# A linear-attention and MLP kernel on one core: five early loads of weights wait for the second one ahead of them, and scaled k gets two lasting buffers

## The chip, the cores and the metric

The kernel runs on one core of one Trainium2 chip. The metric is device time in microseconds, from runs of the whole kernel. Five engines work side by side, each through its own instructions in order: TensorE (PE in the rows, with its weight loads as PEld), VectorE (DVE), ScalarE (ACT), GpSimd (POOL) and SyncE (SP), which issues nearly all DMA transfers here.

## The reference

Per batch (4) and head (8), with a state of 48 x 48 and 768 steps:

```python
for t in range(S):
    cur = np.einsum('bhd,bhe->bhde', u[None] * kt, vt)
    y[:, :, t] = np.einsum('bhd,bhde->bhe', rt, state + cur)
    state = w[None, :, :, None] * state + np.einsum('bhd,bhe->bhde', kt, vt)
...
xt = x.transpose(0, 2, 1)          # x: y with the heads side by side, [4, 768, 384]
h = xt @ U @ V                     # U [768, 32], V [32, 768]: mixes the tokens
u = x + h.transpose(0, 2, 1)
ch = np.maximum(u @ w_ch1, 0.0) @ w_ch2   # 384 -> 1536 -> 384
return (u + ch).astype(np.float32)
```

## The kernel before

**Attention in chunks.** The 768 steps of a batch are cut into 6 chunks of 128, 24 in all. For a chunk, k is scaled by powers of the decay (`ks`, L657 to L663, 8 heads padded from 48 to 64 columns), r and `ks` are turned by TensorE (`ptr`, `ptk`, L712) and scaled on the way out of PSUM (`rT` on VectorE L721, `kT` on ScalarE L727 or VectorE L733). Products of them (`pab`, L751), masked (`am`, L885), multiply v (`pav`, L787 and L793); the state `S` goes from half chunk to half chunk (`S` L913, decayed `SW` L922). The second half of a chunk waits for a one-element copy `seen` (L866) of the first. The step's own term is `dv`: r times k times u (POOL L669 and L671 in the first batch), summed per head (`dg`, VectorE L677) and multiplied by v (ScalarE L681, eight pieces a chunk). `x` (L892) is their sum. The chunks of the first batch come first and have nothing to stand beside.

**The seam.** Each finished chunk of the first batch is multiplied by U into a bank called `wake` (`wake<-x,Uf`, L344), and turned into `pu` (`pu<-ident,x`). When all six are there, the bank is cast to `Gs` (ScalarE L947, VectorE L948), `pu` gets the product of V and `Gs` (`pu<-V,Gs`), and `uTh` and `uTl` (ScalarE L1012, VectorE L1013) are the high and low parts of u for the MLP. Then come the MLP's matmuls (`p<-uTh,w1s` and so on), a group of 384 tokens at a time, with `hh` (ScalarE L1080) and `hl` (VectorE L1081), and the attention of later chunks between them. `wake<-ident` and `wake2<-ident` are fillers, matmuls whose result is not used; the planner puts them where it reckons TensorE would wait. An fp32 matmul stands as two rows (x2) in the trace.

**The weights.** U (1 load unit), V (2), w1 (12 blocks of 128 x 384) and w2 (12) come as 64-bit words; `unit` (L487) makes a load of 384 KB for such a block (`raw_...`, L502) and a conversion to fp32 on ScalarE (L522, L534) and VectorE (L525, L528), after which a cast (ScalarE L548) and a subtraction (VectorE or POOL L549) give high and low parts `w1s`, `w2s`. The load units come in the order u, v_0, v_1, w1_0_0, w1_1_0, w1_2_0, w2_0, w2_1, w2_2, w1_0_1, w1_1_1, w1_2_1, w2_3 and so on. r, k and v of a chunk come as loads of 192 KB (`ldr`, `ldk`, `ldv`, L618) and swapped halves of v (`vsw`, L630).

**What sets the order.** `Plan` (L47 to L273) records all operations with their reads and writes, and a list scheduler orders them on each engine by written-in costs: durations, when a DMA is reckoned to land (`LATE` = 2500 ns more for a load of weights), and how many rows are in flight. Engines then run in that order, waiting only for what they read or write. So a changed cost moves instructions on all engines. `ks` comes from a ring of two buffers (NK = 2), each with a memset of its padding on POOL:

```python
ks = kss[n] = wbuf([128, H, HP], F32, "ks", NK, f"ks_{n}")
op("POOL", 250, lambda: nc.gpsimd.memset(ks.t[:, :, D:], 0.0), [(ks, "pad")], [])
on_either(384, lambda e: e.tensor_mul(ks.t[:, :, :D], kt()[:, :, :D], by_head(tab.t)), [(ks, "d")], kb + [tab],
          only="DVE" if front(n) else None)
```

## Time and profile before

| | |
|---|---|
| Runs | 436.54, 437.32, 436.99 us; median 436.99 |
| Profiled execution, its own time | 439.95 us |
| Its span, first to last instruction | 437.9 us (2.05 us lie around it) |
| Mean granted TensorE clock | 0.984 of full |
| TensorE busy | 419.4 us, 96% of the span |
| VectorE busy | 267.8 us, 61% |
| ScalarE busy | 142.9 us, 33% |
| POOL busy | 55.6 us, 13% |

Busy shares are averages over stages with different limits, so what a change is worth is read from the chain of waits and from windows of the stage that it touches. The granted clock is given as a share of 2.4 GHz; its lower level, 1.2 GHz, is 0.50.

### The profile page before, as it was taken

How to read it: one execution, taken by the hardware profiler on the slowest of the kernel's cores; microseconds unless marked ns; L12 is line 12 of the kernel's file. 1: busy time of each engine (PE TensorE's matmuls, PEld its weight loads, DVE VectorE, ACT ScalarE, POOL GpSimd, SP SyncE). 2: the span in 40 equal slices, each digit the busy share in tenths (PEclk: the TensorE clock that was granted, in tenths of full speed). 3: DMA queues.
4: the chain of work that ended last, by engine and by line, in shares of the span. 5: the costliest groups of instructions: out<-in, count | busy, mean ns of one | idle time of the engine just before them, and what ended most of it. 6: DMA issues, size and time to landing. Idle time of an engine off the chain costs nothing.

```text
span 437.9 us, 12193 instructions
## 1 busy us (share of the span) xinstructions
PE 419.4 (96%) x5125; PEld 399.8 (91%) x5125; DVE 267.8 (61%) x602; ACT 142.9 (33%) x399; POOL 55.6 (13%) x92
## 2 busy tenths in 40 slices
PE   8889999999999999999999999999999999999991
PEld 8678899889999999999999999999999999999991
DVE  6979699999887757767775456567522351122121
ACT  1679679934421213121112221222112131111110
POOL 2651151223110002011100001101100000000000
PEclk9989699999999999999999999999999999999998
DMA  9979999654466876744586653231100510001001
...
DMA packets 178975, 43.93 MB, mean 100 GB/s; under 512 B 168993, under 2 KB 175650, under 8 KB 178914
## 3 DMA queue, kind: packets, MB, share of 16 engines
...
q10 hardware_dynamic: 4752, 0.89, 1.5%
q8 instruction: 42, 0.69, 0.7%
...
## 4 chain that ended last, share of the span: by engine, by line
PE 81%; DVE 8%; ACT 3%; DMA 3%; POOL 1%; issue 1%; SPq 0%; ACTq 0%; DVEq 0%; POOLq 0%
PE p L344 64%; PE pav L787 5%; PE pav L793 4%; PE pu L344 3%; DVE raw_w L528 2%; DVE raw_w L525 2%; PE pab L751 2%; DMA ld<-in_r_dram 1%; DMA ld<-in_v_dram 1%; PE pab L766 1%; PE wake L344 1%; DVE hl L1081 1%; PE pG L958 1%; ACT dv L681 1%; POOL dv L671 1%
## 5 line engine op out<-in xcount | busy, mean ns | idle before, releaser
L344 PE MATMUL p<-uTh,w1s 128*128 128x384 f32 x576 | 148.2, 338 | 0.0
L1081 DVE SCALAR_TENSOR_TENSOR hl<-p,hh 128x384 fp32r<-128x384 f32 x96 | 53.2, 554 | 119.3 <-ACT hh L1080 119.0
L344 PE MATMUL p<-w2s,hh 128*128 128x384 f32 x576 | 120.3, 340 | 0.6 <-ACT hh L1080 0.6
L1080 ACT ACTIVATE hh<-p 128x384 fp32r<-128x384 f32 x96 | 47.2, 491 | 210.3 <-PE p L344 208.7
L344 PEld LDWEIGHTS p<-uTh,w1s 128*128 128x128 f32 x576 | 102.9, 188 | 0.8
L344 PEld LDWEIGHTS p<-w2s,hh 128*128 128x128 f32 x576 | 99.8, 188 | 2.8 <-ACT hh L1080 0.9
L344 PE MATMUL p<-uTl,w1s 128*128 128x384 f32 x288 | 96.4, 335 | 0.0
L344 PE MATMUL p<-w2s,hl 128*128 128x384 f32 x288 | 65.8, 335 | 0.0
L344 PEld LDWEIGHTS p<-uTl,w1s 128*128 128x128 f32 x288 | 54.0, 188 | 0.0
L344 PEld LDWEIGHTS p<-w2s,hl 128*128 128x128 f32 x288 | 51.4, 188 | 0.0
L787 PE MATMUL pav<-vsw,am 64*64 64x48 f32 x384 | 33.0, 226 | 0.6 <-DVE am L885 0.5
L793 PE MATMUL pav<-S,rT 48*64 48x48 f32 x704 | 32.0, 222 | 0.9 <-issue 0.9
L787 PEld LDWEIGHTS pav<-vsw,am 64*64 64x64 f32 x384 | 26.7, 137 | 6.1 <-issue 4.1
L751 PE MATMUL pab<-rT,kT 48*64 48x64 f32 x768 | 31.2, 228 | 0.3 <-DVE rT L721 0.2
L793 PEld LDWEIGHTS pav<-S,rT 48*64 48x64 f32 x704 | 27.9, 139 | 1.0 <-issue 1.0
L751 PEld LDWEIGHTS pab<-rT,kT 48*64 48x64 f32 x768 | 25.1, 137 | 1.5 <-DVE rT L721 0.5
L787 PE MATMUL pav<-ldv,am 64*64 64x48 f32 x320 | 26.5, 222 | 0.0
L787 PEld LDWEIGHTS pav<-ldv,am 64*64 64x64 f32 x320 | 21.5, 134 | 4.7 <-issue 3.9
L885 DVE TENSOR_TENSOR am<-pab,mask 128x256 f32<-128x256 f32 x48 | 19.7, 417 | 6.8 <-PE pav L793 6.2
L661 POOL MEMSET ks<- 128x128 f32 x24 | 4.9, 205 | 133.2 <-PE pab L766 66.8
L766 PE MATMUL pab<-ldv,ks 64*48 64x48 f32 (+1 forms) x576 | 21.0, 212 | 0.0
L926 ACT ACTIVATE SW<-S,wm 112x48 f32<-112x48 f32 x48 | 12.2, 324 | 21.3 <-DVE S L913 20.0
...
## 6 DMA issues: line engine op xcount, KB each, us to landing
raw_w<-in_moe_w_ch_dram SPq DMA_DIRECT2D x24, 384.0 KB, 7.4
out_dram<-x SPq DMA_DIRECT2D x24, 192.0 KB, 2.0
ldr<-in_r_dram SPq DMA_DIRECT2D x20, 192.0 KB, 3.3
ldk<-in_k_dram SPq DMA_DIRECT2D x20, 192.0 KB, 3.6
ldv<-in_v_dram SPq DMA_DIRECT2D x20, 192.0 KB, 3.6
...
```

Of the source, the lines that this page charges most:

```text
L344: return nc.tensor.matmul(*args, **kw)
L525: nc.vector.scalar_tensor_tensor(word(0), word(1), -2 ** 31, word(0), ALU.bitwise_and, ALU.bitwise_or)
L528: nc.vector.scalar_tensor_tensor(word(0), word(1), 3, word(0), ALU.logical_shift_left, ALU.bitwise_or)
L661: op("POOL", 250, lambda: nc.gpsimd.memset(ks.t[:, :, D:], 0.0), [(ks, "pad")], [])
L751: return [lambda q=q, i=i: nc.tensor.matmul(pt.t[(i ^ j) * C2:(i ^ j) * C2 + C2, q * C2:(q + 1) * C2], lhsT=kT.t[rows, q, i * C2:(i + 1) * ...
L766: return nc.tensor.matmul(pt.t[j * HP:j * HP + m, SU + q * D:SU + (q + 1) * D], lhsT=ks.t[half, 2 * q + j, :m], rhs=vt()[half, 2 * q + j, ...
L787: return nc.tensor.matmul(to(q, j, i), lhsT=am[j].t[half, q, :], rhs=vsw[n].t[half, q, :] if j else vt()[half, 2 * q, :], start=(row == RO ...
L793: return nc.tensor.matmul(to(q, row, i), lhsT=rT.t[rows, q, i * C2:(i + 1) * C2], rhs=St[n, i].t[rows, q, :], start=False, stop=(row == RO ...
L885: on_dve(256, lambda e: e.tensor_tensor(am.t, abs_[n][j].t[:, :SU].rearrange("p (h t) -> p h t", h=NP), mask_.unsqueeze(1).broadcast_to([1 ...
L926: nc.scalar.activation(dec.t[:, q], new.t[:, q], AF.Copy, scale=wm.t[:, q])
L1080: on_act(384, lambda: nc.scalar.activation(hh.t, pt.t[:, :TB], AF.Relu), [hh], [pt])
L1081: on_dve(384, lambda e: e.scalar_tensor_tensor(hl.t, pt.t[:, :TB], 0.0, f32(hh.t), ALU.max, ALU.subtract), [hl], [pt, hh])
```

## The change

Two edits. First, `op` and `dma` take an operation `landed`: a load whose landing must come before this one is issued. Loads of weights are counted, and number 7 to 11 (`w2_1`, `w2_2`, `w1_0_1`, `w1_1_1`, `w1_2_1`, counted from u as 0) wait on SP for the load two before them (`w1_2_0`, `w2_0`, `w2_1`, `w2_2`, `w1_0_1`). The planner reckons these five to land 1000 ns late instead of 2500. Second, `ks` alternates between two lasting buffers that are cleared once, whole, at the start.

```diff
@@ Plan.op
+        o.landed = landed
+        if landed:
+            o.behind.add(landed)
@@ Plan.schedule, admit
+            if o.landed:
+                o.ends.append((o.landed.end - o.landed.late, "DMA"))
@@
-    def dma(fn, w_, r_, rows, run, eng="SP", ns=470, dk=0.0, late=0.0, either=False):
+    def dma(fn, w_, r_, rows, run, eng="SP", ns=470, dk=0.0, late=0.0, either=False, landed=None):
...
+    kpad = [cbuf([128, H, HP], F32, f"ks_{i}") for i in range(NK)]
+    for ks in kpad:
+        op("POOL", 250, lambda ks=ks: nc.gpsimd.memset(ks.t, 0.0), [ks], [])
@@
+    PACE = 2
+    PACED = range(7, 12)
+    paced = []
@@ unit
         def load():
+            here = len(paced)
+            before = paced[here - PACE] if here in PACED else None
+            paced.append([None, None])
+            def go(q, p0, ap):
+                i = paced[here][1] = q.dma_start(view(raw.t[p0:p0 + ap.shape[0]]), ap.bitcast(I32) if wide else ap)
+                if before:
+                    tc.add_manual_dep(i.ins, before[1].ins.name,
+                                      mybir.DependencyInfo(mybir.DependencyClass.Sync, mybir.DependencyReason.DATA),
+                                      reason="not too many loads of weights at a time")
             for i, (p0, ap) in enumerate(parts):
-                dma(lambda q, p0=p0, ap=ap: q.dma_start(view(raw.t[p0:p0 + ap.shape[0]]), ap.bitcast(I32) if wide else ap),
-                    [(raw, i)], [], ap.shape[0], (8 if wide else 4) * n, ns=370, late=LATE)
+                paced[here][0] = dma(lambda q, p0=p0, ap=ap: go(q, p0, ap), [(raw, i)], [], ap.shape[0],
+                                     (8 if wide else 4) * n, ns=370, late=1000 if here in PACED else LATE, landed=before and before[0])
@@ a_ks
-        ks = kss[n] = wbuf([128, H, HP], F32, "ks", NK, f"ks_{n}")
-        op("POOL", 250, lambda: nc.gpsimd.memset(ks.t[:, :, D:], 0.0), [(ks, "pad")], [])
+        ks = kss[n] = kpad[n % NK]
```

The planner makes a new order from this. In the rows below, a line number of the changed kernel is 19 to 25 higher than that of the same line before; `x4` counts repeated instructions, and the last number of a name is a running one. Three places follow.

**The turns of chunks 3 and 4 on TensorE, and VectorE beside them.** Before, on TensorE:

```order
L766 MATMUL pab_2_1_463<-ld_2_98,ks_2_258 48x48
L712 MATMUL ptk_3_511<-ident_67,ks_3_408 128x128 x4
L712 MATMUL ptr_3_529<-ident_67,ld_3_106 128x128 x4
L712 MATMUL ptk_4_549<-ident_67,ks_4_534 128x128 x4
L712 MATMUL ptr_4_565<-ident_67,ldr_4_111 128x128 x2
L787 MATMUL pav_2_573<-vsw_2_150,am_2_1_514 64x48
L751 MATMUL pab_3_0_575<-rT_3_557,kT_3_543 64x64
L787 MATMUL pav_2_573<-ld_2_98,am_2_0_499 64x48
```

Now, on TensorE (`ks_0`, `ks_1` are the two lasting buffers):

```order
L736 MATMUL ptk_3_457<-ident_67,ks_1_108 128x128 x2
L811 MATMUL pav_1_416<-ld_1_95,am_1_0_353 64x48
...
L790 MATMUL pab_2_1_470<-ld_2_98,ks_0_100 48x48
L736 MATMUL ptk_3_457<-ident_67,ks_1_108 128x128 x2
L736 MATMUL ptr_3_524<-ident_67,ld_3_106 128x128 x4
L350 MATMUL wake_92<-ident_67 128x128 x2
L736 MATMUL ptk_4_548<-ident_67,ks_0_100 128x128 x4
L811 MATMUL pav_2_562<-vsw_2_150,am_2_1_517 64x48
L775 MATMUL pab_3_0_564<-rT_3_546,kT_3_531 64x64
```

Two of the four turns of `ptk_3` now stand ahead of the second half of chunk 1, a filler stands ahead of `ptk_4`, and the turns of r of chunk 4 come behind the first half of chunk 2. Before, on VectorE:

```order
L913 TENSOR_TENSOR S_2_1_523<-pab_2_1_463,SW_2_1_502 112x192
L892 TENSOR_TENSOR x_1_527<-pav_1_418,dv_1_243 128x384
L922 TENSOR_TENSOR SW_3_0_536<-S_2_1_523,wm_161 112x192
L662 TENSOR_TENSOR ks_4_534<-ldk_4_113,tab_195 128x8x48
L677 TENSOR_REDUCE dg_4_547<-dv_4_497 128x8
L721 TENSOR_TENSOR rT_3_557<-ptr_3_529,tabT_83 112x512
```

Now, on VectorE:

```order
L937 TENSOR_TENSOR S_2_1_527<-pab_2_1_470,SW_2_1_513 112x192
L916 TENSOR_TENSOR x_1_529<-pav_1_416,dv_1_243 128x384
L946 TENSOR_TENSOR SW_3_0_538<-S_2_1_527,wm_161 112x192
L686 TENSOR_TENSOR ks_0_100<-ldk_4_113,tab_195 128x8x48
L745 TENSOR_TENSOR rT_3_546<-ptr_3_524,tabT_83 112x512
L701 TENSOR_REDUCE dg_4_556<-dv_4_504 128x8
```

The scaling `rT_3` has moved ahead of `dg_4`, which reads the `dv_4` of POOL. On POOL itself the memsets of `ks_3` and `ks_4` are gone from between the `dv` of chunks 3, 4 and 5; of their 24 none is left, and two memsets of 128x512 stand at the start.

**The loads on SP.** Before, 17 loads of weights stand in a row, here from the third on to the two loads behind the last:

```order
L502 DMA raw_w1_2_0_684<-in_moe_w_ch1_dram 128x768
L502 DMA raw_w2_0_725<-in_moe_w_ch2_dram 128x768
L502 DMA raw_w2_1_731<-in_moe_w_ch2_dram 128x768
L502 DMA raw_w2_2_735<-in_moe_w_ch2_dram 128x768
L502 DMA raw_w1_0_1_749<-in_moe_w_ch1_dram 128x768
L502 DMA raw_w1_1_1_787<-in_moe_w_ch1_dram 128x768
L502 DMA raw_w1_2_1_792<-in_moe_w_ch1_dram 128x768
...
L502 DMA raw_w2_7_858<-in_moe_w_ch2_dram 128x768
L618 DMA ldr_6_670<-in_r_dram 128x8x48
L618 DMA ldk_6_552<-in_k_dram 128x8x48
```

Now, from the third on:

```order
L521 DMA raw_w1_2_0_679<-in_moe_w_ch1_dram 128x768
L521 DMA raw_w2_0_688<-in_moe_w_ch2_dram 128x768
L643 DMA ldr_6_691<-in_r_dram 128x8x48
L643 DMA ldk_6_551<-in_k_dram 128x8x48
L643 DMA ldv_6_786<-in_v_dram 128x8x48
L521 DMA raw_w2_1_801<-in_moe_w_ch2_dram 128x768
L521 DMA raw_w2_2_812<-in_moe_w_ch2_dram 128x768
L655 DMA vsw_6_822<-in_v_dram 64x4x48 x2
L643 DMA ldk_7_734<-in_k_dram 128x8x48
L655 DMA vsw_7_850<-in_v_dram 64x4x48
L643 DMA ldr_7_890<-in_r_dram 128x8x48
L521 DMA raw_w1_0_1_911<-in_moe_w_ch1_dram 128x768
```

Of the seventeen only four come first; r, k and v of chunk 6 stand ahead of `w2_1`, the loads of chunk 7 ahead of `w1_0_1` and more of them ahead of `w1_2_1`, which stands six places further on. All later weights come behind that one.

**The seam, on ScalarE and TensorE.** Before, on ScalarE, from the last `seen` of the first batch on:

```order
L866 COPY seen_5_997<-pav_5_973 1x1
L548 CAST w1s_2_0_999<-raw_w1_2_0_684 128x384
L534 ACTIVATE raw_w1_1_1_787<-raw_w1_1_1_787 128x384
L522 ACTIVATE raw_w1_2_1_792<-raw_w1_2_1_792 128x384
L548 CAST w2s_0_1026<-raw_w2_0_725 128x384
L534 ACTIVATE raw_w1_2_1_792<-raw_w1_2_1_792 128x384
L522 ACTIVATE raw_w2_2_735<-raw_w2_2_735 128x384
L534 ACTIVATE raw_w2_2_735<-raw_w2_2_735 128x384
L947 CAST Gs_0_1047<-wake_92 96x384
L548 CAST w2s_1_1052<-raw_w2_1_731 128x384
L522 ACTIVATE raw_w2_3_799<-raw_w2_3_799 128x384
...
L1012 CAST uTh_0_0_1067<-pu0_0_0_855 128x384
```

Now, on ScalarE:

```order
L890 COPY seen_5_980<-pav_5_959 1x1
L547 ACTIVATE raw_w1_0_1_911<-raw_w1_0_1_911 128x384
L559 ACTIVATE raw_w1_0_1_911<-raw_w1_0_1_911 128x384
L705 ACTIVATE dv_6_903<-ldv_6_786,dg_6_1021 128x48 x8
L971 CAST Gs_0_1059<-wake_92 96x384
L559 ACTIVATE raw_w1_1_1_938<-raw_w1_1_1_938 128x384
L573 CAST w1s_0_0_1072<-raw_w1_0_0_661 128x384
L573 CAST w1s_1_0_1076<-raw_w1_1_0_669 128x384
L573 CAST w1s_2_0_1083<-raw_w1_2_0_679 128x384
L1036 CAST uTh_0_0_1088<-pu0_0_0_848 128x384
...
L573 CAST w2s_0_1104<-raw_w2_0_688 128x384
```

The conversion of `w1_0_1` and the eight pieces of `dv_6` now stand between `seen_5` and `Gs`, and one weight pass and three casts between `Gs` and the first `uTh`. On VectorE the join of `raw_w1_1_1` and three subtractions stand between `Gs` and `uTl`, where one `raw_w` operation stood. Before, on TensorE, from `wake` of chunk 5 on:

```order
L344 MATMUL pu0_1_2_970<-ident_67,x_4_968 128x128
L344 MATMUL wake_92<-x_5_1029,Uf_794 96x128 x3
L344 MATMUL wake2_1041<-ident_67 128x128
L344 MATMUL pu0_1_0_1021<-ident_67,x_5_1029 128x128
L344 MATMUL pu0_1_1_1024<-ident_67,x_5_1029 128x128
L344 MATMUL pu0_1_2_970<-ident_67,x_5_1029 128x128
L344 MATMUL wake2_1041<-ident_67 128x128 x2
L344 MATMUL pu0_0_0_855<-V3_817,Gs_0_1047 128x384
```

Now, on TensorE:

```order
L350 MATMUL pu0_1_1_1007<-ident_67,x_4_956 128x128
L350 MATMUL wake_92<-x_5_1011,Uf_744 96x128 x3
L350 MATMUL wake2_1040<-ident_67 128x128
L350 MATMUL pu0_1_2_1013<-ident_67,x_4_956 128x128
L350 MATMUL pu0_1_0_1005<-ident_67,x_5_1011 128x128
L350 MATMUL pu0_1_1_1007<-ident_67,x_5_1011 128x128
L350 MATMUL pu0_1_2_1013<-ident_67,x_5_1011 128x128
L350 MATMUL wake2_1040<-ident_67 128x128 x7
L350 MATMUL pu0_0_0_848<-V3_799,Gs_0_1059 128x384
```

Seven fillers stand ahead of the first product with `Gs` where two stood, and one more turn of x behind `wake` of chunk 5. Further on, between the last `uTh` and the first `hh` of the next group of tokens, ScalarE has 30 passes and casts and one set of `dv` pieces, where it had 27 and two sets. VectorE has 77 rows between the last `uTl` and the `kT` of chunk 8 in both orders.

## Rows read from the trace of the kernel before

**Rows 1.** The profile's page: the span; busy us (share of the span) and instructions of each engine; from its list of DMA issues the load of r of a chunk (count, KB each, median us from issue to landing).

```profile
span 437.9 us, 12193 instructions
...
PE 419.4 (96%) x5125; PEld 399.8 (91%) x5125; DVE 267.8 (61%) x602; ACT 142.9 (33%) x399; POOL 55.6 (13%) x92
...
ldr<-in_r_dram SPq DMA_DIRECT2D x20, 192.0 KB, 3.3
```

**Rows 2.** The chain that ended last, in order of time: start us, us, engine and what. Pieces from the whole span.

```profile
8.91 6.24 DMA ld<-in_r_dram
...
33.60 0.57 ACT raw_v L534
...
49.03 2.43 PE pu L344 x10
...
51.46 1.71 PE wake L344 x8
...
55.16 1.06 PE pu L344 x6
...
56.22 0.24 PE wake L344 x2
...
56.49 1.28 ACT uTh L1012 x3
...
57.77 0.45 ACT w1s L548
...
71.10 0.47 ACT hh L1080
...
71.60 0.56 DVE hl L1081
...
97.62 0.61 DVE kT L733
...
98.93 3.16 PE p L344 x18
...
341.42 87.62 PE p L344 x505
```

**Rows 3.** Windows of the span: from:to, us, then busy us (and instructions) of TensorE, its weight loads, VectorE, ScalarE and POOL, the granted clock (PEclk), the DMA share and GB/s.

```profile
24.00:26.00 2.00, 0.45 (x5) 0.22 (x2) 1.39 (x4) 1.99 (x10) 1.92 (x2) 1.00 0.69 129
28.00:30.00 2.00, 2.00 (x60) 1.58 (x52) 0.54 (x3) 1.84 (x8) 1.56 (x2) 0.50 1.16 245
30.00:32.00 2.00, 2.00 (x69) 1.93 (x68) 1.75 (x5) 0.60 (x3) 1.25 (x4) 0.76 0.75 212
50.00:52.00 2.00, 2.00 (x11) 2.00 (x11) 1.50 (x4) 0.23 (x1) 0.00 (x0) 0.50 1.08 347
54.00:56.00 2.00, 2.00 (x13) 2.00 (x12) 1.33 (x2) 1.24 (x4) 2.00 (x2) 0.78 0.95 301
72.00:98.00 26.00, 24.75 (x300) 22.96 (x298) 25.97 (x54) 19.27 (x50) 6.85 (x8) 1.00 0.64 95
100.00:420.00 320.00, 320.00 (x3748) 307.70 (x3748) 177.19 (x395) 71.20 (x193) 22.07 (x37) 1.00 0.39 75
```

**Rows 4.** POOL in order of time: start us, us, line, operation, tile; in brackets idle time before it and what ended that.

```profile
1.08 0.20 POOL L661 MEMSET ks<- 128x128 f32 x1
...
23.64 1.00 POOL L669 TENSOR_TENSOR dv<-ldr,ldk 128x384 f32<-128x384 f32 x1 [1.56 <-DVE dg L677]
24.72 1.53 POOL L671 TENSOR_TENSOR dv<-dv,ub 128x384 f32<-128x384 f32 x1
26.19 0.20 POOL L661 MEMSET ks<- 128x128 f32 x1
```

**Rows 5.** VectorE in order of time, same columns.

```profile
24.84 0.55 DVE L662 TENSOR_TENSOR ks<-ldk,tab 128x384 f32<-128x384 f32 x1
26.28 0.55 DVE L677 TENSOR_REDUCE dg<-dv 128x8 f32<-128x384 f32 x1 [0.89 <-POOL dv L671]
26.75 0.68 DVE L721 TENSOR_TENSOR rT<-ptr,tabT 112x512 f32<-112x512 f32 x1
...
53.29 0.55 DVE L948 TENSOR_TENSOR Gs<-wake,Gs 32x384 fp32r<-32x384 f32 x1 [1.78 <-ACT Gs L947]
```

**Rows 6.** TensorE in order of time, same columns.

```profile
26.45 0.66 PE L712 MATMUL ptk<-ident,ks 128*128 128x128 f32 x4 [1.99 <-POOL ks L661]
```

**Rows 7.** ScalarE in order of time, same columns.

```profile
52.78 0.47 ACT L947 CAST Gs<-wake 96x384 fp32r<-96x384 f32 x1 [2.55 <-PE wake L344]
...
55.37 2.40 ACT L1012 CAST uTh<-pu 128x384 fp32r<-128x384 f32 x6 [0.76 <-PE pu L344]
...
67.58 1.90 ACT L681 ACTIVATE dv<-ldv,dg 128x48 f32<-128x48 f32 x8
```

**Rows 8.** DMA issues in three short windows (32 to 33, 45 to 45.5 and 63.9 to 64.3 us): count, KB each, median us from issue to landing.

```profile
raw_w<-in_moe_w_ch_dram SPq DMA_DIRECT2D x2, 384.0 KB, 3.6
...
raw_w<-in_moe_w_ch_dram SPq DMA_DIRECT2D x1, 384.0 KB, 8.1
...
raw_w<-in_moe_w_ch_dram SPq DMA_DIRECT2D x1, 384.0 KB, 3.9
```

**Rows 9.** SP's queue in order of time: start us, us, count.

```profile
32.16 13.22 SPq L502 DMA_DIRECT2D raw_w<-in_moe_w_ch_dram  x17
```

More of the change, by code (lines that the diff above doesn't have):

```diff
@@ L74, in __init__, with op @@
         self.clocks = {}
-    def op(self, eng, ns, fn, w=(), r=(), alt=(), lock=False, dma=0.0, rows=0, late=0.0, tiled=False, dk=0.0):
+    def op(self, eng, ns, fn, w=(), r=(), alt=(), lock=False, dma=0.0, rows=0, late=0.0, tiled=False, dk=0.0, landed=None):
         if self.direct:
@@ L362, in one_of @@
         return op(*first[:3], w_, r_, lock=first[3], alt=alt, dk=dk)
-    def dma(fn, w_, r_, rows, run, eng="SP", ns=470, dk=0.0, late=0.0, either=False):
+    def dma(fn, w_, r_, rows, run, eng="SP", ns=470, dk=0.0, late=0.0, either=False, landed=None):
         q = nc.scalar if eng == "ACT" else nc.sync
         return op(eng, ns, lambda: fn(q), w_, r_, dma=rows * max(1.08 if run < 500 else 0.96, run / 400),
-                  rows=rows, late=late, dk=dk, alt=[("ACT", ns, lambda: fn(nc.scalar), False)] if either else ())
+                  rows=rows, late=late, dk=dk, landed=landed, alt=[("ACT", ns, lambda: fn(nc.scalar), False)] if either else ())
     ident_ = const.tile([128, 128], F32, name="ident")
```

## The prediction

> **What bounds the kernel now.** I read the page first. TensorE is busy for 419.4 of 437.9 us and VectorE for 267.8 [rows 1]. That is an average over stages, so the chain that ended last comes next, read by time [rows 2]. It shows four stretches. Up to about 49 us it runs through the attention of the first batch and the conversion of U and V on ScalarE. From 49.03 to 56.49 it is TensorE at the seam between that attention and the first MLP block. From 56.49 ScalarE and then, from 71.60, VectorE carry it, up to the `kT` of 97.62. From 98.93 on it is MLP matmuls to the end. The reader should see that only the part up to 98 us can be shortened: from 100 to 420 us TensorE is busy for 320.00 of 320.00 us at the full clock [rows 3], and the order there is nearly unchanged. The windows show the rest: VectorE has 25.97 of 26.00 us between 72 and 98, and the clock falls to its half level (1.2 of 2.4 GHz) twice, 0.50 at 28 to 30 us and 0.50 at 50 to 52 us, having been at 1.00 in 24 to 26 us, while TensorE was busy for 0.45 of 2.00 us.
>
> **Part 1: the padding memsets.** For chunk 4 TensorE's turn of `ks` waited 1.99 us, put down to the memset of the padding [rows 6]. The memset ended at 26.39; it is 0.20 us long, but POOL works in order and it stood behind the `dv` of chunk 4, 24.72 to 26.25 [rows 4]. The product itself, on VectorE, was done at 25.39 [rows 5]. With the memset gone the turn may start about 26.39 - 25.39 = 1.0 us earlier. In the new order `rT_3` also stands ahead of the `dg` that waits for that `dv`; it stood at 26.75 behind a `dg` at 26.28, and can now follow the product at 25.39 directly, 1.3 us earlier. So the attention half that follows starts by 1.0 to 1.3 us earlier, and perhaps without the fall of the clock at 28 us. The bounds for this place: 0, if `kT` on ScalarE ends as late as before, and 3 us if the clock stays up as well (two stretches at 0.50 and 0.76 [rows 3], 4.0 us, whose work at full clock would be 0.50 x 2 + 0.76 x 2 = 2.5 us, so 1.5 more).
> How much survives? At 33.60 the chain is in `raw_v` on ScalarE [rows 2], the conversion of a load of V, which nothing in this change lets land earlier. I let 0.5 us survive at the end of the attention, between 0 and 1.5. It does not enter the sum by itself, because in the new order `Gs` waits on ScalarE for something else (part 2).
> The other memsets were later and stood in POOL's idle time; removing them is worth nothing. If that cover went, it would be 0.20 us each. The two memsets of whole buffers at the start stand where one of 0.20 us stood at 1.08 us [rows 4]. With four times the elements each takes between 0.2 and 0.8 us. The chain there waits for the load of r until 8.91 + 6.24 = 15.15 us [rows 2], so they cost nothing. The two buffers change hands as the ring of two did.
>
> **Part 2: the paced loads.** Before, SP issued 17 loads of weights in a row from 32.16 us, over 13.22 us [rows 9]. The first took 3.6 us from issue to landing, the last 8.1 [rows 8]: they land from about 35.8 to 53.3 us, 17.5 / 16 = 1.09 us apart, so the third (`w1_2_0`) at 38.0 and the fourth (`w2_0`) at 39.1. Now the fifth, `w2_1`, may be issued only at 38.0, the sixth, `w2_2`, at 39.1, and behind them on SP in order stand r, k, v and the swapped v of chunks 6 and 7 and all later weights. A lone load late in the program took 3.9 us [rows 8]; with eight in flight it took 8.1. These are my bounds for each paced load.
> - `w2_1`: 41.9 to 46.1. Three loads of 192 KB, median 3.3 us [rows 1], go just ahead of it; I take 44.
> - `w2_2`: about 45.
> - `w1_0_1`, issued when `w2_1` has landed: 47.9 to 52.1. With the loads of chunk 7 before it but no row of weights, it is nearer to the 3.9; I take 48.7.
> - `w1_1_1` about 49.7; `w1_2_1` about 53.
> The Trainium skill, "DMA: Bandwidth & Descriptors", section "Anatomy of one DMA — SWDGE (gpsimd) path", speaks against the change here: a transfer costs a fixed 2.0 us plus its bytes at 436 GB/s, so few transfers in flight leave the fixed part uncovered. By its figures a 384 KB load takes an estimated 2.9 us and two in flight give one per 1.45 us, so five loads would be 5 x (1.45 - 1.09) = 1.8 us late. The trace's lone 3.9 us is longer than that; no row of before shows two in flight alone.
> Who waits for these? On ScalarE, in order, `raw_w1_0_1` (two passes) and the eight `dv_6` pieces now stand ahead of the cast of `Gs`. Two passes are 0.9 us (a 128x384 pass is 0.45 [rows 2]) and eight pieces 1.90 [rows 7]. So `Gs` starts at 48.7 + 0.9 + 1.9 = 51.5 us instead of 52.78 [rows 7]. Behind it stand one pass of `raw_w1_1_1` and three casts of weights, 4 x 0.45 = 1.8, so the casts `uTh` can start at 51.5 + 0.45 + 1.8 = 53.8 us instead of 55.37. The six `uTh` take 2.40, and in the new order two casts of `w2` stand among them, 0.9: the last ends at about 57.1, where before it ended at 57.77 [rows 7]. **-0.6 us.** On VectorE the join of `raw_w1_1_1` and three subtractions now stand before `uTl`, some 4 x 0.55 us (0.55 is `Gs` there [rows 5]) from 52.1 on, done at 54.3, so `uTl` still waits for `uTh`.
> Further on, ScalarE has between the last `uTh` and the first `hh` of the next group of tokens two more weight passes but one set of eight `dv` pieces fewer: 3 x 0.45 - 1.90 = **-0.5 us**, and ScalarE is what the chain shows there until 71.10. VectorE has as many instructions as before between the last `uTl` and the `kT` of 97.62: 0. From there on TensorE's work is as before: 0.
>
> **Part 3: the fillers.** At the seam the new order has one filler, a turn of x more after it, and seven fillers between `wake` of chunk 5 and the first product with `Gs`, against one and two. A filler is two of the trace's rows: 0.24 us at full clock (56.22) and 2 x 1.71 / 8 = 0.43 at half [rows 2]. Five more are 1.2 to 2.1 us. I cost them at nothing, since `Gs` is the wait that ends last: TensorE would, with the attention's end 0.5 us earlier and the full clock, reach the product near 53 us, just behind `Gs`. If the clock is at half there, the cover is gone (rival two).
>
> **Sum.** 0 (memsets) - 0.6 - 0.5 + 0 = -1.1 us: 439.95 - 1.1 = 438.85 us for the profiled execution. That one stands 439.95 - 436.99 = 2.96 us above the median of the runs, so the forecast is **435.9 us**. A measurement of this kernel can tell about 0.2%, 0.87 us, from no change.
>
> **The rivals.**
> *One: more gain.* The loads come at their lower bound (47.9, 0.8 earlier) and the clock stays up in both places. For it: both falls come with a TensorE that waits, and the 1.99 us wait goes. Against: the V loads at 33.60. It would be -1.1 - 0.8 - 0.8 (of the 1.5 at 28 us): about 434.2 us.
> *Two: nothing is left, because the clock stays at half at the seam.* Then TensorE sets the pace: five turns and `wake` as slow as before, 0.5 us earlier, a turn and five fillers more, 6 x 0.24 to 6 x 0.43 = 1.4 to 2.6, so the product with `Gs` comes at about 55.16 - 0.5 + 1.4 = 56.1, 0.9 later, less the 0.5 on ScalarE: +0.4. For it: the rows of before at 0.50 to 0.78 [rows 3]. Against: more fillers were put there and earlier loads reach TensorE sooner. About 437.3 us. The same would come of waits that bind nothing, if `w1_2_0` and `w2_0` had landed when SP gets to `w2_1`; against that, the fifth of 17 issues over 13.22 us came at about 35.5, ahead of 38.0.
> *Three: slower, since a late load holds `Gs`.* ScalarE cannot go past `raw_w1_0_1`. The point that decides: `Gs` is as early as before if `w1_0_1` lands by 52.78 - 1.9 - 0.9 = 50.0 us. At the upper bound, 52.1, `Gs` starts at 54.9, `uTh` at 57.2, and the last of these ends at 60.5 us: +2.7 - 0.5 = +2.2, or 439.2; with a landing of 51.5 it is 438.6. For it: SP is in order, and every paced load is a wait for all issues behind it. Against: the lone 3.9 us.
>
> **How the numbers follow.** Forecast 0.40 (434.9 to 436.1); rival one 0.12 (434.2), two 0.23 (436.2 to 437.8), three 0.25 (437.9 to 439.2). The bounds of the landing decide most, and 50.0 lies in the middle of 47.9 to 52.1, though I take the lower half. Faster: 0.40 + 0.12 = 0.52; within 0.2%: 0.23; slower: 0.25. The likeliest case's own range is 434.9 to 436.1; the range given, 434.0 to 438.9, leaves out the last part of rival three and little of rival one.
>
> **What would show it.** Right: no wait of TensorE on POOL near 26 us; the clock at 1.00 from 28 to 30; `raw_w1_0_1` starting on ScalarE near 48.7 without a long wait behind a DMA; `Gs` near 51.5; the last `uTh` near 57.1; the first long row of MLP matmuls about 1 us before 98.93. Wrong: ScalarE idle ahead of `raw_w1_0_1` after 50.0, a clock of 0.50 at 50 us with the product with `Gs` after 55.16, or a VectorE stretch to `kT` longer than the 26 us between 72 and 98, which would make the gains of the seam worthless.

## The result

The changed kernel takes 440.72 us (median of 20 runs, 439.31 to 443.59), the kernel before 437.56 in the same session (20 runs): a ratio of 1.0065, 95% interval 1.005 to 1.0081. It is slower by some 2.9 us, where 1 us faster was forecast. Runs of one kernel lie up to 4 us apart, with the stretches in which the clock falls, so traces are compared below at like clocks.

The page of the profiled execution (its own time 442.01 us), which answers to [rows 1]:

```profile
span 440.3 us, 12210 instructions
...
PE 419.6 (95%) x5149; PEld 400.7 (91%) x5149; DVE 268.5 (61%) x612; ACT 138.4 (31%) x379; POOL 55.9 (13%) x68
```

TensorE's work is the same. ScalarE has 20 instructions fewer, VectorE ten more, and GpSimd 24 fewer, nearly all of them memsets. The windows of the span, columns as in [rows 3], with one stretch added:

```profile
28.00:30.00 2.00, 2.00 (x73) 1.82 (x72) 1.97 (x5) 1.96 (x9) 1.47 (x2) 1.00 0.77 219
...
50.00:52.00 2.00, 2.00 (x9) 2.00 (x10) 1.89 (x4) 1.46 (x5) 0.00 (x0) 0.50 1.07 245
...
72.00:98.00 26.00, 23.13 (x242) 21.75 (x241) 22.63 (x50) 19.12 (x48) 11.42 (x8) 1.00 0.69 125
...
40.00:56.00 16.00, 14.41 (x232) 13.38 (x231) 13.25 (x25) 9.27 (x26) 4.74 (x6) 0.79 0.92 239
...
0.00:40.00 40.00, 32.15 (x708) 28.85 (x708) 33.25 (x96) 25.35 (x90) 15.20 (x27) 1.00 0.95 179
40.00:101.08 61.08, 56.62 (x636) 53.87 (x634) 53.97 (x112) 43.72 (x110) 19.49 (x18) 0.94 0.81 197
```

The clock no longer falls at 28 us. Between 72 and 98 us VectorE now has 3.4 us of idle time, and GpSimd 11.42 us of work instead of 6.85. In 40 to 56 us ScalarE is busy for 9.27 us. The kernel before, in the same windows, at the same mean clock of 0.79 in 40 to 56:

```profile
40.00:56.00 16.00, 15.10 (x234) 14.19 (x234) 11.50 (x25) 11.23 (x26) 3.49 (x4) 0.79 1.01 354
...
0.00:40.00 40.00, 33.33 (x700) 29.72 (x700) 32.19 (x91) 24.62 (x89) 17.23 (x36) 0.96 0.95 183
40.00:98.22 58.22, 55.32 (x618) 51.97 (x617) 53.39 (x108) 44.93 (x113) 14.98 (x18) 0.94 0.83 204
```

The last window of each runs to the end of `kT` of chunk 8 on VectorE, 98.22 us before and 101.08 after: the whole loss is there by then. The chain that ended last, after, shows what stood in the way; [rows 2] answer to it:

```profile
40.46 6.33 DMA raw_w<-in_moe_w_ch_dram
...
49.99 2.43 PE pu L350 x10
...
55.32 1.56 PE wake L350 x14
56.88 1.06 PE pu L350 x6
...
83.94 2.19 POOL w1s L574
...
89.81 2.71 POOL w2s L574
```

Three things are new in it: a load of a weight at 40.46, fillers at 55.32, and GpSimd at 83.94 and 89.81. ScalarE and then GpSimd in order of time:

```profile
45.62 0.56 ACT L547 ACTIVATE raw_w<-raw_w 128x384 int32<-128x384 uint8 x1 [3.54 <-DMA raw_w<-in_moe_w_ch_dram]
...
50.54 0.56 ACT L547 ACTIVATE raw_w<-raw_w 128x384 int32<-128x384 uint8 x1 [2.54 <-DMA raw_w<-in_moe_w_ch_dram]
51.00 0.55 ACT L559 ACTIVATE raw_w<-raw_w 128x384 f32<-128x384 f32 x1
51.45 1.89 ACT L705 ACTIVATE dv<-ldv,dg 128x48 f32<-128x48 f32 x8
53.74 0.47 ACT L971 CAST Gs<-wake 96x384 fp32r<-96x384 f32 x1 [0.40 <-PE wake L350]
...
59.49 0.89 ACT L1036 CAST uTh<-pu 128x384 fp32r<-128x384 f32 x2
...
78.16 0.49 ACT L1104 ACTIVATE hh<-p 128x384 fp32r<-128x384 f32 x1
...
92.55 0.55 ACT L573 CAST w2s<-raw_w 128x384 fp32r<-128x384 f32 x1 [2.81 <-POOL w2s L574]
```

```profile
79.18 1.04 POOL L574 TENSOR_TENSOR w2s<-raw_w,w2s 128x384 fp32r<-128x384 f32 x1 [2.09 <-ACT w2s L573]
80.97 2.31 POOL L574 TENSOR_TENSOR w2s<-raw_w,w2s 128x384 fp32r<-128x384 f32 x1 [0.75 <-ACT w2s L573]
...
83.94 2.18 POOL L574 TENSOR_TENSOR w1s<-raw_w,w1s 128x384 fp32r<-128x384 f32 x1 [0.51 <-ACT w1s L573]
...
89.81 2.70 POOL L574 TENSOR_TENSOR w2s<-raw_w,w2s 128x384 fp32r<-128x384 f32 x1 [3.69 <-ACT w2s L573]
```

ScalarE stands for 3.54 and 2.54 us on loads, the second ahead of `Gs`. Later, GpSimd's subtractions of `w2_7`, `w1_0_3` and `w2_8` take 2.2 to 2.7 us each instead of 1.04, and ScalarE's next cast waits up to 2.81 us for one. SP's queue, for [rows 9]:

```profile
31.75 2.02 SPq L521 DMA_DIRECT2D raw_w<-in_moe_w_ch_dram  x4
33.90 0.38 SPq L643 DMA_DIRECT2D ldr<-in_r_dram  x1
34.38 1.11 SPq L643 DMA_DIRECT2D ldk<-in_k_dram  x1
35.54 4.15 SPq L643 DMA_DIRECT2D ldv<-in_v_dram  x1
39.79 1.05 SPq L521 DMA_DIRECT2D raw_w<-in_moe_w_ch_dram  x2
...
45.78 1.74 SPq L521 DMA_DIRECT2D raw_w<-in_moe_w_ch_dram  x2
...
51.62 4.35 SPq L521 DMA_DIRECT2D raw_w<-in_moe_w_ch_dram  x9
```

SP issues `w2_1` at 39.79, not 38.0, as it stands for 4.15 us at the load of v ahead of it. Nine weights come only at 51.62. For [rows 6], and the `kT` of chunk 8 on VectorE:

```profile
26.00 0.66 PE L736 MATMUL ptk<-ident,ks 128*128 128x128 f32 x4 [1.05 <-DVE ks L686]
```

```profile
100.41 0.67 DVE L757 TENSOR_TENSOR kT<-ptk,wi 112x512 f32<-112x512 f32 x1
```

**A mark in time.** In 18 of the 19 traces that have `kT` of chunk 8 on VectorE, the turns of x of the second batch begin 50.1 to 51.0 us after that `kT` ends, and from there to the end of the span it is 289.2 us within 0.5. So the end of that `kT` marks where a kernel stands in time, though it need not be what TensorE waits for. (e2 has this `kT` on ScalarE; e18 is the one exception, told there.) The way to it falls into three pieces, as in the prediction: to the end of the last `uTh` on ScalarE, from there to the first `hh` of the next group of tokens (the seventh `hh` of the trace), and from there to the end of `kT` of chunk 8.

| trace | clock below 0.97 in, up to 100 us | last `uTh` ends | seventh `hh` | `kT_8` ends | VectorE busy + idle up to it |
|---|---|---|---|---|---|
| before | 26 to 32, 48 to 56 | 57.77 | 77.18 | 98.22 | 85.58 + 12.64 |
| e8, before again | 26 to 34 | 55.20 | 75.85 | 96.90 | 85.35 + 11.55 |
| e12 | nowhere | 54.05 | 74.47 | 95.33 | 86.49 + 8.84 |
| after | 46 to 56 | 60.38 | 78.16 | 101.08 | 87.22 + 13.86 |
| e15, after again | 34 to 38 | 57.53 | 75.57 | 98.44 | 88.46 + 9.98 |
| e6 | nowhere | 57.72 | 75.92 | 98.84 | 86.02 + 12.82 |
| e9 | 16 to 26, 48 to 56 | 60.40 | 78.19 | 99.16 | 89.45 + 9.71 |
| e13 | 32 to 38 | 57.11 | 76.44 | 100.43 | 86.53 + 13.90 |
| e17 | 48 to 52 | 58.88 | 79.35 | 101.73 | 87.39 + 14.34 |
| e18 | 26 to 32, 48 to 52, 98 on | 56.45 | 75.84 | 100.59 | 88.29 + 12.30 |

The clock is read in windows of 2 us. e12 is the kernel before with two late subtractions moved, so up to about 80 us it is a third trace of that kernel, and the only one of them with the clock up throughout. The rows of the seventh `hh` before, and of the seam in e12, on ScalarE:

```profile
77.18 0.47 ACT L1080 ACTIVATE hh<-p 128x384 fp32r<-128x384 f32 x1
```

```profile
49.99 0.48 ACT L951 CAST Gs<-wake 96x384 fp32r<-96x384 f32 x1 [0.36 <-PE wake L348]
...
51.72 2.33 ACT L1016 CAST uTh<-pu 128x384 fp32r<-128x384 f32 x6
```

From the first trace of either kernel, both with the clock low at the seam, the last `uTh` is 2.6 us later, the piece behind it 1.6 us shorter (19.4 to 17.8) and the last piece 1.9 us longer (21.0 to 22.9). With the clock up at the seam (e8 and e12 against e15 and e6) the last `uTh` is 2.3 to 3.7 us later, the middle piece 2.2 to 2.6 shorter, and the last one again 1.8 to 2.1 longer.

### The profile page after: what moved, and what is told of

Same layout as the page of the kernel before. It is cut to its first block, busy times and chain, and to the rows that moved or that the text cites. A ratio compares the mean times of both kernels' runs of the same rounds, so it can differ in the third digit from the quotient of the medians.

```text
span 440.3 us, 12210 instructions
## 1 busy us (share of the span) xinstructions
PE 419.6 (95%) x5149; PEld 400.7 (91%) x5149; DVE 268.5 (61%) x612; ACT 138.4 (31%) x379; POOL 55.9 (13%) x68
## 4 chain that ended last, share of the span: by engine, by line
PE 81%; DMA 5%; ACT 4%; DVE 3%; POOL 2%; SPq 2%; issue 1%; DVEq 0%; POOLq 0%
PE p L350 65%; PE pav L811 4%; PE pav L817 3%; PE pu L350 3%; SPq L643 2%; PE pab L775 2%; DMA raw_w<-in_moe_w_ch_dram 1%; DMA ld<-in_k_dram 1%; PE pab L790 1%; DMA ub<-in_u_dram 1%; ACT raw_w L559 1%; PE wake L350 1%; POOL w2s L574 1%; ACT raw_w L547 1%; DMA wT<-in_w_dram 1%
## 5 line engine op out<-in xcount | busy, mean ns | idle before, releaser
L775 PE MATMUL pab<-rT,kT 48*64 48x64 f32 x768 | 30.3, 224 | 1.4 <-DVE rT L745 1.3
L686 POOL TENSOR_TENSOR ks<-ldk,tab 128x384 f32<-128x384 f32 x13 | 13.4, 1031 | 115.5 <-PE pab L790 59.3
L790 PEld LDWEIGHTS pab<-ldv,ks 64*48 64x48 f32 (+1 forms) x576 | 18.6, 128 | 0.0
```

Of the source, the lines that this page charges most:

```text
L775: return [lambda q=q, i=i: nc.tensor.matmul(pt.t[(i ^ j) * C2:(i ^ j) * C2 + C2, q * C2:(q + 1) * C2], lhsT=kT.t[rows, q, i * C2:(i + 1) * ...
L790: return nc.tensor.matmul(pt.t[j * HP:j * HP + m, SU + q * D:SU + (q + 1) * D], lhsT=ks.t[half, 2 * q + j, :m], rhs=vt()[half, 2 * q + j, ...
```

## The experiments

**Either half of the change, alone.** e1 has the buffers of `ks` and the old loads, e2 the paced loads and the old `ks`; the planner lays out each anew.

```
e1, against before
+    kpad = [cbuf([128, H, HP], F32, f"ks_{i}") for i in range(NK)]
-        ks = kss[n] = wbuf([128, H, HP], F32, "ks", NK, f"ks_{n}")
-        op("POOL", 250, lambda: nc.gpsimd.memset(ks.t[:, :, D:], 0.0), [(ks, "pad")], [])
+        ks = kss[n] = kpad[n % NK]
e2, against before: unit() and dma() of the changed kernel
```

> The two lasting buffers without the waits; the planner puts the loads of weights in the order of before. If the loss comes from the loads (theories A and B below), this has none of it: the turn of ks of chunk 4 no longer waits for POOL, 0 to 1 us of that is left at the end, 436.5 to 437.6 us where before stands at 437.56. If it came from the whole new order around the turns, 440 or more. Theory A: the new order puts r, k and v of chunk 6 ahead of w2_1 on SP, whose queue stands on the third of them for 4.15 us, so the weights land late whether they wait or not. Theory B: the waits for the second load ahead hold the weights back. Theory C: the late weights cost little, the extra fillers at the seam cost the time.

> The waits with the ring of two and its 24 memsets, so the first half of the change is undone. A, B and C: the whole loss or a little more, 440.3 to 441.8 us against 437.56 before; A names w2_1 issued at about 39.8, B and C do not.

Measured: e1 439.67, 1.004 (1.0008 to 1.0071); e2 440.49, 1.007 (1.0044 to 1.0096). Each is slower alone. So neither half can be left out to save the other, and the two losses do not add. In e1 the weights come as early as before (355 GB/s from 40 to 56 us, 354 before), so a new order by itself can cost time.

**Waits, fillers and the planner's delay.** e3 keeps the changed order and drops the waits; e4 has fewer fillers at the seam; e5 tells the planner 4500 ns for a paced load.

```
e3:  -                if before:
     +                if False:
e4:  +        seam = [w for w in self.woken if w[1] is self.wakes[1][2]]
     +        cut = seam[3:8] + seam[9:]
     +        self.woken = [w for w in self.woken if w not in cut]
e5:  -  late=1000 if here in PACED
     +  late=4500 if here in PACED
```

> The changed kernel with its order on every engine, but the five loads do not wait for the second load ahead. A: SP still stands on v of chunk 6 till about 39.7 and w2_1 lands at about 45.6; only w1_0_1 may be issued up to 1.2 us earlier: 439.5 to 441 us. B: w2_1 and what follows land up to 4 us earlier, 436.5 to 438 us.

> The changed kernel with 4 fillers fewer ahead of the first product with Gs and 3 fewer behind the last, everything else in its order. C: Gs is ready at 54.8 and the product came at 56.9, so 4 fillers at 0.22 us and 3 more give back 1.5 us or more: 439.2 or less. A and B: 0.4 to 1.2 us, 439.5 to 440.3, since the attention still ends about 1 us late and the casts of weights on ScalarE are in the way.

> The changed kernel with the planner's figure for the landing of the five paced loads at 4500 ns late in place of 1000. SP's order stays, so the weights land as late as in the changed kernel; but on ScalarE seen of chunk 5 now stands ahead of the conversions of w2_1 and w2_2, and Gs ahead of that of w1_0_1. Theory A1: the loss is ScalarE's order, engines held behind loads that the planner reckoned too early: 436.5 to 438.3 us against 440.72 of the changed kernel and 437.6 of before. Theory A2: the late loads themselves cost, since ScalarE and VectorE are idle ahead of the seam and have the conversions left for the stretch in which they are full: 439.3 to 441 us.

Measured: 439.87, 1.006 (1.0037 to 1.0084); 440.16, 1.0049 (1.0023 to 1.0075); 439.99, 1.0051 (1.0026 to 1.0076). The waits themselves cost nothing that shows: without them SP still stands at that load of v, for 3.83 us, and issues the next two weights at 38.45. e4 is not told from the changed kernel by its interval, so the runs show no gain from fewer fillers.

**The place of the loads on SP.** Both without waits, in the order and sharing out of the changed kernel: e6 issues the five weights right behind `w2_0`; e7 moves r, k and v of chunk 6 behind `w2_2`.

```
e6:  +        for i in range(7, 12):
     +            self.paced[i][0].start = self.paced[6][0].start + 0.01 * (i - 6)
e7:  +        for i, o in enumerate(self.moved):
     +            o.start = self.paced[8][0].start + 0.01 * (i + 1)
```

> The changed kernel with its order on all engines but SP: there the five loads stand right behind w2_0, ahead of r, k and v of chunk 6, and wait for nothing. They land from about 40 to 44 us as before. A1 and A2 alike: the loss goes, 436.3 to 438.3 us. If the loss came from the rest of the new order (fillers, dv of chunk 6 ahead of Gs, casts ahead of uTh), it stays: 439.3 us or more.

> The changed kernel with r, k and v of chunk 6 behind w2_2 on SP, and no waits. w2_1 and w2_2 land at about 40 to 42 us instead of 45.6 and 46.8, w1_0_1 and the rest as late as in the changed kernel. A1: seen of chunk 5 is not held, 1 us of the loss goes, but Gs stands behind w1_0_1 still: 439 to 440 us. A2: a part only, in the share of two loads of five: 439 to 440 us.

> The kernel before once more, for a second trace of it: where the granted clock stays at 1.00 around 28 and 50 us the MLP part starts about 2 us earlier than in the first trace (103.16 us for the first long row), and its time is near 436.5 us.

Measured: e6 441.0, 1.0074 (1.0045 to 1.0102); e7 439.66, 1.0053 (1.0032 to 1.0074); e8, one run, 438.9. In e6 ScalarE no longer stands on a load of a weight between 40 and 58 us, and nothing is won. But e6 has put another late load in the place of the weights: k of chunk 6, now behind them, takes 7.32 us from 38.41 in the chain that ended last, and `dv_6`, which stands ahead of `Gs`, waits for the `dg` that depends on it:

```profile
49.82 1.91 ACT L707 ACTIVATE dv<-ldv,dg 128x48 f32<-128x48 f32 x8 [2.62 <-DVE dg L703]
51.76 0.48 ACT L973 CAST Gs<-wake 96x384 fp32r<-96x384 f32 x1
```

`Gs` at 51.76 is earlier than 52.78 [rows 7], where the clock was low, but 1.8 us later than e12's 49.99 at the full clock. So e6 shows that these five loads are not the only thing that makes the seam late; it does not show that a late load costs nothing there.

**GpSimd's late subtractions.** Four of them to VectorE in the changed kernel (e9); three to GpSimd in the kernel before (e10); two to VectorE in e1's kernel (e11) and two in the kernel before (e12).

```
+        for name in (...):
+            o = self.subs[name]
+            o.fn = [w[2] for w in o.ways if w[0] == "DVE"][0]
e9: w2s_7, w1s_0_3, w2s_8, w2s_10    e10 ("POOL"): w2s_7, w1s_0_3, w2s_8
e11: w1s_0_3, w1s_2_3                e12: w2s_6, w1s_1_3
```

> The changed kernel with its order, but the last four subtractions of weights that the planner gave to POOL (w2_7, w1_0_3, w2_8, w2_10, at 80 to 97 us) are done by VectorE at the same places. New theory D: raw words and split weights share a ring of 25 buffers, so near the end of the conversion each cast on ScalarE waits for a subtraction to release a raw buffer; on POOL these took 2.31, 2.18 and 2.70 us (0.55 on VectorE), ScalarE waited 0.68, 0.46 and 2.81 us for them, and VectorE, full in the kernel before between 72 and 98 us, is idle for 3.3 of 16 us. D: 1.5 to 3 us less than the changed kernel, 437.7 to 439.3. If the loss is made ahead of 60 us: no gain, 440 to 441.

> The kernel before with its order, but three late subtractions (w2_7, w1_0_3, w2_8), on VectorE there, are done by POOL. D: 1.5 to 3.5 us slower than before, 438.8 to 441. If the late subtractions don't matter: as before, 437 to 438, or faster by the 1.4 us that VectorE is spared in a stretch in which it is full.

> The two lasting buffers alone (439.67 us, with loads in the order of before), with its last two subtractions (w1_0_3, w1_2_3: 2.23 and 2.71 us on POOL) on VectorE. D: 1 to 3 us less, 436.5 to 438.7. Otherwise 439 to 440.

> The kernel before with its last two subtractions on POOL (w2_6, w1_1_3: 1.05 and 1.15 us) on VectorE. D: POOL's was 0.5 us longer each and ScalarE waited 1.26 us behind the second; VectorE has 1.1 us more in a full stretch. 0.8 less to 0.6 us more: 436.5 to 438.

Measured: e9 440.95, 1.0084 (1.0056 to 1.0112); e10 440.09, 1.005 (1.0025 to 1.0075); e11 438.94, 1.0028 (1.0002 to 1.0055); e12 436.7, 0.9974 (0.9942 to 1.0006). Late subtractions on GpSimd cost: e10 is 2.7 us slower than the kernel before it was run beside. The last piece of the table shows it in the traces: in e9 it takes 20.98 us, in the changed kernel 22.91 and before 21.05; in e10 it takes 22.18; in e11 20.52 against 22.01 in e1. In e9 VectorE's idle time between 76 us and `kT_8` falls from 3.4 to 0.2 us, and with the last `uTh` where the changed kernel has it, `kT_8` ends 1.9 us earlier. The median of e9's ten runs does not show that gain, which stays open; five of them have a mean clock of 0.985 or less, against one in twenty of the changed kernel's. e12 may be a gain; its interval does not exclude none.

**The order at `Gs`.** In e13 `w1_0_1` and `w1_1_1` stand behind `Gs`, and `dv` of chunks 6 and 7 behind the last `uTh` and `uTl`; e14 is e13 with e9's four subtractions and e4's fillers; e15 is the changed kernel again. e16 is the kernel before in its own order with e12's two subtractions, two lasting buffers and no memsets.

```
e13: +        for i, name in enumerate([(w, i) for w in ("w1_0_1", "w1_1_1") for i in range(3 if w == "w1_1_1" else 4)]):
     +            k[name].start = max(k[name].start, gs + 0.01 * (i + 1))
     +        for i, name in enumerate([("dvs", 6), ("dv0", 7), ("dv1", 7)]):
     +            k[name].start = max(k[name].start, late + 0.01 * (i + 1))
e16: -        op("POOL", 250, lambda: nc.gpsimd.memset(ks.t[:, :, D:], 0.0), [(ks, "pad")], [])
     +        ks.twin = kpad[n % NK]
     +        op("POOL", 250, (lambda: nc.gpsimd.memset(ks.t, 0.0)) if n < NK else (lambda: None), [(ks, "pad")], [])
```

> The changed kernel with its order and its waits, but on ScalarE the conversion of w1_0_1 and dv of chunk 6 stand behind Gs (dv behind the last uTh), on VectorE the operations of w1_0_1 and w1_1_1 and dv of chunk 7 behind Gs. Theory E: Gs, which needs only the attention, is held in the engines' order behind work on loads that come late; at equal clocks it was cast at 52.1 us (r, k, v of chunk 6 moved) against 50.0 in the kernel before, and the six uTh after it took 3.3 us against 2.4. E: 1.2 to 2.2 us less than the changed kernel, 438.3 to 439.7. Otherwise 440 to 441.5.

> The run before this one, and the last four subtractions of POOL on VectorE, and 7 fillers fewer at the seam; waits and the order on SP stay. E and D together hold the loss (E 1.2 to 2.2, D 1.9 as the traces of e9 and the changed kernel show, fillers 0.5): 436.0 to 438.0. If the late loads cost by themselves: 438.5 or more.

> The changed kernel once more, beside the two runs above on the same chip: 440 to 441.5 us.

> The kernel before with its order on every engine, the two lasting buffers cleared at the start and no memset of padding later, and its last two subtractions of POOL on VectorE (the latter alone gave 436.7 against 437.4). If the wait of 1.99 us for the memset reaches the end, 0.5 to 1 us less than that: 435.5 to 436.3; if the conversion of V behind it takes it up, 436.3 to 437.0.

Measured: e13 441.19, 1.0083 (1.0053 to 1.0113); e14 440.89, 1.0083 (1.0054 to 1.0111); e15 439.93, 1.0052 (1.0023 to 1.008); e16 437.26, 0.9984 (0.9964 to 1.0003), against 0.9974 for e12. e13 casts `Gs` early, as ScalarE in order of time shows:

```profile
50.29 0.47 ACT L980 CAST Gs<-wake 96x384 fp32r<-96x384 f32 x1 [3.64 <-PE wake L358]
...
56.24 0.87 ACT L1046 CAST uTh<-pu 128x384 fp32r<-128x384 f32 x2
```

`Gs` comes 2.5 us earlier than in the first trace of the kernel before, whose clock was low there, and about where e12 has it (49.99). But the last `uTh` ends at 57.11, where it ends at 54.05 in e12 and 55.20 in e8: the fillers and the casts of `w1` and `w2` still stand between. So e13 does not mend the seam; it wins nothing, and neither does e14. e16 shows that the 1.99 us wait for the memset [rows 6] was worth nothing that can be measured.

**The sharing out among the engines, both ways.** Between 35 us and `kT_8`, 22 operations are on other engines in the changed kernel than before. e17 puts them back in the changed kernel (with e13's order at `Gs`, and four instructions on the decay's range behind `kT_8` again); e18 puts the kernel before's 22 where the changed kernel has them, with all its loads as early as ever, and these four instructions ahead of `kT_8`.

```
e17, against e13
+        put = {
+            "DVE": [254, 281, 320, 362, 435, 569, 698, 722, 745, 800],
+            "POOL": [286, 332, 368, 452, 523, 615, 728],
+            "ACT": [363, 487, 583, 662, 717],
+        }
+        for eng, numbers in put.items():
+            for n in numbers:
+                self.ops[n].fn = [w[2] for w in self.ops[n].ways if w[0] == eng][0]
e18, against before: the same the other way, DVE 12, POOL 7, ACT 3, and
+        for i, n in enumerate((1040, 1041, 1042, 1043)):
+            self.ops[n].start = self.ops[607].start - 0.04 + 0.01 * i
+        self.ops[1039].start = 86000
```

> The changed kernel with its loads, waits and order of the program kept, but 22 operations between 35 us and kT of chunk 8 put back on the engine that has them in the kernel before (ten to VectorE, seven to GpSimd, five to ScalarE; among them the four late subtractions of w2_7, w1_0_3, w2_8 and w2_10, which go from GpSimd to VectorE, and the byte operations of three weights, which go from VectorE to ScalarE); the four instructions on the decay's range stand behind kT of chunk 8 again, and w1_0_1, w1_1_1 and dv of chunks 6 and 7 stand behind Gs and the first uTl, as in e13. Theory that the sharing out of the work among VectorE and GpSimd costs the time: VectorE has five instructions fewer ahead of kT of chunk 8 than in the changed kernel (some 2.4 us) and no idle time between 80 and 96 us (3.4 us there in the changed kernel), so 2 to 3.5 us come back: ratio 1.000 to 1.004, and the seam of the second batch is at 146 to 148. Rival, that the loads which land 4 us later cost it whatever engine does the work: the time stays, 1.005 to 1.008.

> The converse: the kernel before with its loads, memsets and order kept, and the same 22 operations put on the engines that have them in the changed kernel, with the four instructions on the decay's range ahead of kT of chunk 8. No load waits for another and every weight lands as early as before. Theory of the sharing out: VectorE has six instructions more ahead of kT of chunk 8 (some 2.9 us) and GpSimd has the four late subtractions, so 2 to 3.5 us are lost: ratio 1.005 to 1.008. Rival, late loads: no change, 0.998 to 1.002. Second rival, that both are needed: this one and e17 both lie between, 1.001 to 1.005.

Measured: e17 442.2, 1.0107 (1.0064 to 1.015); e18 443.88, 1.0128 (1.0086 to 1.0169). The converse loses more than was expected, and the undoing does not bring the time back. e18's windows:

```profile
96.00:100.00 4.00, 1.20 (x57) 1.07 (x56) 3.90 (x7) 0.68 (x2) 1.83 (x3) 0.93 0.40 74
100.00:104.00 4.00, 3.35 (x12) 3.36 (x13) 4.00 (x10) 1.01 (x4) 0.00 (x0) 0.50 0.00 0
```

`kT_8` ends 3.0 us later than the mean of the two traces of before (97.56), with every weight landing early. VectorE's rows ahead of it:

```profile
97.01 0.54 DVE L1092 SCALAR_TENSOR_TENSOR hl<-p,hh 128x384 fp32r<-128x384 f32 x1
97.47 1.19 DVE L481 TENSOR_SCALAR wrc<-wrow 1x384 f32<-1x384 f32 x1
98.69 0.55 DVE L482 TENSOR_TENSOR wrc<-wrc,wrow 1x384 f32<-1x384 f32 x1
99.28 0.54 DVE L483 TENSOR_REDUCE outside<-wrc 1x1 f32<-1x384 f32 x1
...
99.92 0.67 DVE L744 TENSOR_TENSOR kT<-ptk,wi 112x512 f32<-112x512 f32 x1
```

From 97.47 to 99.92 VectorE is on the four instructions on the decay's range, while TensorE, whose next turn of r starts at 100.65 after a wait of 3.45 us, waits for `kT_8` behind them. That is 2.45 us of the 3.0. TensorE (1.20 of 4.00 us busy) then runs at the half level, which is the other 2.6 us of e18's loss. So e18 shows what VectorE's work costs right ahead of a `kT` that TensorE waits for; how much of its 1.3% comes from the 22 operations it does not show. In the changed kernel three of the four stand there too (1.28 us of VectorE's time), but TensorE does not wait for `kT_8` there.

In e17 it is ScalarE that is full, as it also is before and after from 64 to 80 us: its busy time is the fourth of each window. VectorE in order of time follows.

```profile
72.00:80.00 8.00, 7.45 (x45) 7.09 (x44) 7.48 (x12) 8.00 (x24) 3.13 (x3) 1.00 0.79 166
80.00:88.00 8.00, 6.37 (x39) 5.71 (x38) 6.64 (x15) 8.00 (x22) 1.57 (x3) 1.00 0.69 108
```

```profile
52.67 0.55 DVE L991 TENSOR_TENSOR Gs<-wake,Gs 32x384 fp32r<-32x384 f32 x1 [2.26 <-ACT Gs L990]
...
90.79 0.56 DVE L593 TENSOR_TENSOR w1s<-raw_w,w1s 128x384 fp32r<-128x384 f32 x1 [1.49 <-ACT w1s L592]
...
100.58 0.56 DVE L1125 SCALAR_TENSOR_TENSOR hl<-p,hh 128x384 fp32r<-128x384 f32 x1 [0.77 <-ACT hh L1124]
```

VectorE's idle time there ends with ScalarE each time. So the theory that the sharing out alone is the cause falls too: with late loads the new sharing stands 0.65% above the kernel before, and the old one, in e13's order, 1.1%.

## Why the prediction was wrong

**Where the time went.** The forecast had three terms up to `kT_8`: -0.6 to the last `uTh`, -0.5 on ScalarE behind it, 0 on VectorE to `kT_8`. The first traces show +2.6, -1.6 and +1.9, which is the 2.9 us by which `kT_8` is late (98.22 to 101.08); behind it these two traces give back 0.5. The +1.9 has an experiment: with the four late subtractions on VectorE it is gone (e9: 20.98 us against 22.91). The late seam has none that brings it back: in e4, e6, e7 and e13, which have the clock up there, the last `uTh` ends at 57.1 to 58.5, against 54.05 to 55.20 in e12 and e8.

**What the late loads do.** The windows from 40 to 56 us, at like clocks, show 354 GB/s before and 239 after, at 0.79; and, with the clock at 1.00 throughout, 349 in e8 and 256 in e15:

```profile
40.00:56.00 16.00, 15.18 (x252) 13.99 (x253) 14.51 (x32) 14.38 (x35) 2.96 (x4) 1.00 0.98 349
```

```profile
40.00:56.00 16.00, 15.42 (x260) 13.97 (x258) 15.78 (x30) 11.99 (x34) 4.86 (x6) 1.00 0.95 256
```

115 GB/s over 16 us is 1.84 MB, four to five weights of 384 KB that have not come by 56 us. Without them ScalarE does 2.0 us less in these 16 us (11.23 to 9.27) in the one pair and 2.4 (14.38 to 11.99) in the other. From 64 to 80 us ScalarE is full in both kernels (15.94 and 15.91 us), so it cannot catch up there. In the new plan VectorE has nine instructions more ahead of `kT_8`, 3.6 us by their rows: two byte passes and a `kT` among them, and 1.4 us for the three on the decay's range. VectorE's busy time up to there is 85.5 us in the two traces of before and 87.0 in the mean of seven traces with the new list (85.76 to 88.46). But the sum of its work does not set the end: e12 has 86.49 us of work and the earliest `kT_8`, while e5, run from a plan of its own, has 85.43 and `kT_8` at 97.96. What differs most at like clocks is idle time, 8.84 us in e12 against 12.82 in e6.

Late weights are not needed for a loss, since e1 loses 0.4% with all of them early, and whether they are the root here is not shown: a plan with the weights early and all the rest as changed was not run. So the traces show where the time went, and for the last piece why. Why the seam is late stays open: late loads, more work on VectorE ahead of `uTl`, casts of weights ahead of and among the `uTh`, and fillers all stand there, and no run takes all of them away.

**Step by step.**
- *Part 1* was right in its mechanism. TensorE's turn of `ks` of chunk 4 waits for VectorE alone and starts at 26.00, not 26.45, and the clock stays at 1.00 at 28 us. It is 0.45 earlier and not 1.0 to 1.3, because `ks` itself came at 25.40 on VectorE instead of 24.84 [rows 5]. That it adds 0 to the sum agrees with e16.
- *Part 2, the landings*: 44, 45, 48.7 and 49.7 were forecast; ScalarE's rows put them just before 45.62, 46.81 and 50.54. The two that had bounds lie in their upper half. The forecast had SP at `w2_1` by 38.0, with only the wait to hold it; the three loads of 192 KB ahead of it held SP itself until 39.79.
- *Part 2, "the last ends at about 57.1 [...] -0.6 us"* is the first step that failed: the last `uTh` ends at 60.38, 2.6 us later than before. `w1_0_1` landed at about 50.5, not 48.7; `Gs` was cast at 53.74, not 51.5, at the end 0.40 us behind TensorE's `wake`; and `uTh` then waited 1.08 us for TensorE, which was still among fillers at the half clock (the chain has 1.56 us of them from 55.32).
- *Part 2, ScalarE behind it, -0.5*: -1.6 in the first traces. (The text says two weight passes more and its sum takes three; the rows of the order, 30 against 27, give three.)
- *Part 2, "VectorE has as many instructions as before between the last `uTl` and the `kT` of 97.62: 0"* is the second. It is true of the count, and it counts instructions where it should have priced waits. From the seventh `hh` to `kT_8` it takes 22.91 us instead of 21.05. The step did not ask which engine the subtractions of the last stretch are on: on GpSimd they made 3.4 us of idle time on VectorE, in a stretch of which the prediction itself says that VectorE has 25.97 of 26.00 us. Counted from the last `uTl`, as the step says, the stretch is only 0.4 us longer (39.46 to 39.82); that is luck, as ScalarE's gain lies in it too. Nor does it see the nine instructions more that stand ahead of the last `uTl` (net: two passes over `raw_w` tiles, three `SW`, two `dv`, a `dg`, a subtraction), where the prediction took VectorE to be waiting for ScalarE anyway.
- *Part 3* is not settled: e4 shows no gain from fewer fillers, but in the profiled run `uTh` waited behind them at a clock of 0.50, the condition of rival two.
- *The rivals.* Three named the side and the late load, and its 2.2 us were near the 2.9. `w1_0_1` did land after 50.0 us, and the last `uTh` came at its price, 60.5. That is luck in part: by its working `Gs` is at 54.9, and here `Gs` was earlier and the fillers of rival two made up the rest; and it has nothing for the last piece. The three signs that would prove the prediction wrong all came: ScalarE idle until 50.54, a clock of 0.50 at 50 us with the product with `Gs` after 55.16, and a longer VectorE stretch to `kT`.
